# Retention in a three-stage kernel: scores on quarters of TensorE's array, and ahead of the preceding chunk's state part

## The chip, the cores and the metric

The kernel runs on one core of a Trainium2 chip. The metric is the device time of one execution in microseconds (us), as the median of several executions.

## The reference, cut to what matters

Three stages follow one another: a retention layer (2 sequences, 8 heads, 768 steps, head size 64), a mixture of 8 experts with one expert for each token, and a second mixture of 4 experts in which every expert sees every token. The change is in the first.

```python
gamma = 1.0 - 2.0 ** (-5.0 - np.arange(H))
for t in range(S):
    state = gamma[None, :, None, None] * state + np.einsum('bhd,bhe->bhde', k[:, :, t], v[:, :, t])
    y[:, :, t] = scale * np.einsum('bhd,bhde->bhe', q[:, :, t], state)
x = y.transpose(0, 2, 1, 3).reshape(B * S, H * D)
x = moe(x)      # gate: argmax of x @ w_gate; relu(x @ w1[e]) @ w2[e] for the chosen expert
return moe2(x)  # sum over the 4 experts, weighted with the given probabilities
```

All inputs and the output are float32.

## The kernel before, in words

Retention is computed in chunks of 128 steps, 6 of each sequence, 12 in all (NT = 12, NCH = 6). A chunk is numbered i, and c = i % 6 is its place in its sequence. For each chunk there are five pieces of TensorE work, each on all 8 heads:

- S (`st_S`): scores, keys times queries within the chunk. 8 matmuls of 64 x 128 weights against 128 columns: a pair of heads lies on the two halves of the 128 partitions, so the two matmuls of a pair use the two row halves of the array and write two PSUM banks, S_0 and S_1. VectorE multiplies them with the causal mask into `sd` (L251).
- U (`st_U`): keys times values, added up over the chunks of a sequence in one bank that is held (64 columns, 128 x 64 weights, two column halves). ScalarE copies it to `st`, the state (L275). The last chunk of a sequence has no U.
- I (`st_I`): queries times the state of the chunks before, 64 x 64 weights, on quarters of the array, into the banks O_0 and O_1. The first chunk of a sequence has no I.
- O (`st_O`): `sd` times values, 128 x 64 weights (two column halves), added onto I in the same banks. ScalarE copies the two banks to `ot` (L315), GpSimd (POOL) multiplies it with the decay to `xT` (L316); for the last two chunks VectorE does both in one step (L320).
- X (`x_pe`): `xT` times a matrix that transposes it and computes the gate's logits, 128 x 128 weights, into the two held banks x0 and x1. VectorE reduces the logits (L359, L367), ScalarE copies the rest to `xk` (L363) and sends it to memory.

From the logits VectorE finds each token's expert (`x_dve`: `cd` L376, `cm`, `ohs`, `cum`, `ohk`). R (`r_pe`) is two small matmuls that count the tokens ahead of each token; VectorE reads them (`r_dve`: `sel` L403, then `at` L418), and `g_pe` (slot) adds up the table of slots. POOL also makes `vg`, the scaled values (L230).

The loop over `it` issues for each iteration I, U, O and the xT step of chunk it-1, `vg` of chunk it+1, S of chunk it, the loads of chunk it+3, then X of chunk it-2, slot of it-4 and R of it-3 with VectorE's two chains braided: cd, sel, cm, at, ohs, cum, ohk. The engines run in the order in which the program issues (a manual schedule), each at its own pace, and semaphores keep them apart. The loads of q and k (`qk`), k and v (`kv`) go out on SyncE's queue three chunks ahead.

PSUM: O, S and R take their banks from four in turn (`bank`: `banks[nbank[0] % 4]`), so five allocations in an iteration go round four banks; a bank can be written again when its last reader is done. U, slot and X have banks of their own.

A float32 matmul stands in the trace as two weight loads and two matmul records; S of a chunk so has 16 of each. In the order lists below it is one row.

Of the kernel before, what the change touches and what calls it, by code (L numbers as in the profile page):

```python
# [20 lines left out]
P = 128  # L21
# [11 lines left out]
FMAX = 3.4028234663852886e38  # L33
PASS = ((0, 0), (0, 1), (1, 0))
WARM0 = 9
DEPTH = 4
HT = 384
NS = 2 * E2 * 4
# [17 lines left out]
def tile_retention_moe_moe(ctx: ExitStack, tc, qkv, cst, gqt, a1, a2, b1, b2, out, cap):  # L56
# [20 lines left out]
    def bank(name, tag=None):  # L77
        if tag is None:
            tag = banks[nbank[0] % len(banks)]
            nbank[0] += 1  # L80
        return ps[0].tile([P, 512], F32, tag=tag, name=name)

    def warm(n, fill):
        bk = bank("warm")
        for _ in range(n):
            nc.tensor.matmul(out=bk, lhsT=fill[:, 0:P], rhs=fill, start=True, stop=True)
# [20 lines left out]
    def load_w(upto):  # L107
        while nload[0] < min(upto, len(rawof)):
            u = rawof[nload[0]]
            raws[u] = pr.tile([P, 1024], F32, tag="raw", name=f"raw{nload[0]}")  # L110
            nc.sync.dma_start(out=raws[u], in_=wsrc(u))
            nload[0] += 1
# [63 lines left out]
    with ExitStack() as actx:  # L176
# [19 lines left out]
        def load_qk(i):  # L196
            qk_t[i] = pq.tile([P, 2, 512], F32, tag="qk", name=f"qk{i}")
            nc.sync.dma_start(out=qk_t[i], in_=qkv[i, :, 0:1024])

        def load_kv(i):  # L200
            kv_t[i] = pq.tile([P, 2, 512], F32, tag="kv", name=f"kv{i}")
            nc.sync.dma_start(out=kv_t[i], in_=qkv[i, :, 1024:2048])

        def load_gq(c):
            nc.sync.dma_start(out=gqs[:, c], in_=gqt[c])
# [13 lines left out]
        load_kv(2)  # L219
        warm(WARM0, fill)  # L220
        nc.gpsimd.memset(zero, 0.0)
# [5 lines left out]
        def st_v(i):  # L227
            kv = kv_t.pop(i)
            vg = p2.tile([P, 8, HD], F32, tag="vg", name=f"vg{i}", bufs=3)
            nc.gpsimd.tensor_tensor(  # L230
                out=vg, in0=kv[:, 1].rearrange("p (h d) -> p h d", h=8),
                in1=gk[:, i % NCH].rearrange("p (h d) -> p h d", d=1).to_broadcast([P, 8, HD]),
                op=ALU.mult,
            )
            live[i] = {"vg": vg, "k": kv[:, 0]}

        def st_S(i):
            qk = qk_t.pop(i)
            sd = p2.tile([P, 2, 512], F32, tag="sd", name=f"sd{i}")
            live[i].update(sd=sd, q=qk[:, 0])  # L240
            bks = [bank(f"S{i}_{j}") for j in range(2)]
            for hp in range(4):
                cols = slice(hp * P, (hp + 1) * P)
                for j in range(2):
                    r = slice(64 * j, 64 * j + 64)
                    nc.tensor.matmul(  # L246
                        out=bks[j][:, cols], lhsT=qk[r, 1, cols], rhs=qk[r, 0, cols],
                        start=True, stop=True,
                    )
            for j in range(2):  # L250
                nc.vector.tensor_tensor(  # L251
                    out=sd[:, j].rearrange("p (h t) -> p h t", h=4),
                    in0=bks[j].rearrange("p (h t) -> p h t", h=4), in1=causal, op=ALU.mult,
                )
# [3 lines left out]
        def st_U(i):  # L258
            c = i % NCH
            if c == NCH - 1:  # L260
                return
            if c == 0:
                u_ps[0] = bank(f"U{i}", "u")
            u = u_ps[0][:, 0:KD * HD].rearrange("p (a d) -> p a d", a=KD)
            k = live[i].pop("k")
            vg = live[i]["vg"]
            for hp in range(4):
                for j in range(2):
                    h = 2 * hp + j
                    nc.tensor.matmul(  # L270
                        out=u[64 * j:64 * j + 64, hp], lhsT=k[:, h * HD:(h + 1) * HD],
                        rhs=vg[:, h], start=(c == 0 and hp == 0),
                        stop=True, skip_group_check=True,
                    )
            nc.scalar.copy(st[(c + 1) % 2], u)  # L275
# [5 lines left out]
        def st_I(i):  # L281
            c = i % NCH
            live[i]["o"] = [bank(f"O{i}_{j}") for j in range(2)]
            q = live[i].pop("q")
            if c > 0:
                for hp in range(4):
                    for j in range(2):
                        r = slice(64 * j, 64 * j + 64)
                        nc.tensor.matmul(
                            out=o_at(i, hp, j), lhsT=st[c % 2][r, hp],  # L290
                            rhs=q[r, hp * P:(hp + 1) * P], start=(hp < 2), stop=False,
                            skip_group_check=True,
                        )

        def st_O(i):
            d = live[i]
            c = i % NCH
            sd, vg = d.pop("sd"), d.pop("vg")
            for hp in range(4):
                for j in range(2):  # L300
                    nc.tensor.matmul(  # L301
                        out=o_at(i, hp, j), lhsT=vg[:, 2 * hp + j],
                        rhs=sd[:, j, hp * P:(hp + 1) * P], start=(c == 0 and hp < 2), stop=True,
                        skip_group_check=True,
                    )

        def st_x(i):
            d = live[i]
            c = i % NCH
            bks = d.pop("o")  # L310
            xT = p2.tile([P, 512], F32, tag="xT", name=f"xT{i}")
            if i < NT - 2:
                ot = p2.tile([P, 512], F32, tag="ot", name=f"ot{i}")
                for j in range(2):
                    nc.scalar.copy(ot[:, 256 * j:256 * j + 256], bks[j][:, 0:256])  # L315
                nc.gpsimd.tensor_tensor(out=xT, in0=ot, in1=gqs[:, c], op=ALU.mult)  # L316
            else:
                for j in range(2):
                    cols = slice(256 * j, 256 * j + 256)
                    nc.vector.tensor_tensor(  # L320
                        out=xT[:, cols], in0=bks[j][:, 0:256], in1=gqs[:, c, cols], op=ALU.mult
                    )
            d["xT"] = xT
# [98 lines left out]
        def g_pe(i):  # L422
            at = ats.pop(i)
            for b in range(SL // P):
                nc.tensor.matmul(
                    out=slot_ps[:, b], lhsT=at[:, b * P:(b + 1) * P], rhs=ohk[:, i],
                    start=(i == 0 and b == 0), stop=True, skip_group_check=True,
                )
# [6 lines left out]
                        seqs.remove(q)  # L435

        for it in range(NT):
            if it >= 1:
                st_I(it - 1)
                st_U(it - 1)  # L440
                st_O(it - 1)
                st_x(it - 1)
            for i in range(it + 1 if it else 0, min(it + 2, NT)):
                st_v(i)
            st_S(it)
            if it + 3 < NT:
                load_qk(it + 3)
                if it + 2 < NCH:
                    load_gq(it + 2)
                load_kv(it + 3)  # L450
            if it == 5:
                nc.sync.dma_start(out=xd[0:1], in_=zero)
            if it == 2:
                nc.vector.tensor_copy(ub, kc[:, 0:P])
                nc.vector.tensor_copy(ident, iw[:, 0, 0:P])
            if it >= 6:
                load_w(max(nload[0], min(4, it - 5)))
            seqs = []
            if it >= 2:
                x_pe(it - 2)  # L460
                if it >= 4:
                    g_pe(it - 4)
                seqs.append(x_dve(it - 2))
            if it >= 3:
                r_pe(it - 3)
                seqs.append(r_dve(it - 3))
            braid(*seqs)
            if it == 8:
                split_w(0)
# [11 lines left out]
        for b in range(SL // P):  # L481
            nc.gpsimd.indirect_dma_start(
                out=xe0[:, b], out_offset=None, in_=xd[0:1 + NE * P],
# [40 lines left out]
        for ks in (range(2), range(2, KD)):  # L524
# [3 lines left out]
            out=cnt[:, 0], in0=cps, scalar1=float(cap), scalar2=None, op0=ALU.min  # L528
        )
        nc.vector.tensor_tensor(out=cnt[:, 1], in0=cps, in1=cnt[:, 0], op=ALU.subtract)  # L530
        if general:
            nc.vector.tensor_scalar(
                out=nbf, in0=cnt[:, 0], scalar1=float(SM), scalar2=None, op0=ALU.is_gt
            )
            for j in range(1, NB):
                nc.vector.scalar_tensor_tensor(
                    out=nbf, in0=cnt[:, 0], scalar=float(SM + j * P), in1=nbf,
# [200 lines left out]
    def upto(u):  # L738
        ahead = DEPTH + sum(u >= v for v in (5, 7, 29, 31)) - sum(u >= v for v in (W0 - 6, W0 - 5))
        while nsplit[0] <= min(u + ahead, W0 + 3):  # L740
            split_w(nsplit[0])
            nsplit[0] += 1
# [125 lines left out]
    for e in range(E1):  # L868
        x = xet.pop(e)
        hs = []  # L870
        for c in range(4):
# [6 lines left out]
            for ff, k in order:  # L878
# [12 lines left out]
                out=hl, in0=t, scalar=0.0, in1=hh.bitcast(F32), op0=ALU.max, op1=ALU.subtract  # L891
# [413 lines left out]
```

## Time and profile before

| | us |
|---|---|
| median of 3 runs | 744.73 (744.6 to 744.79) |
| the profiled execution | 744.18 |
| its span | 742.4 |
| retention, up to the first expert's product | 68.1 |

The span is what the trace covers. Times in the rows are microseconds from its start. PE stands for TensorE's matmuls and PEld for its weight loads, DVE is VectorE, ACT ScalarE, POOL GpSimd, SP SyncE (SPq its DMA queue). L251 is line 251 of the kernel. A matmul's end is modelled in the trace, so the parts of TensorE's work are told apart here by the start of their first weight load. A row of the timeline merges like instructions that follow one another: start, time that they took together, engine, line, operation, output <- input, array form (weight rows * columns), shapes, count, and in brackets the idle time before it and what ended it.

### The profile page before, as it was taken

The numbers are of one execution on the slowest core, as the hardware profiler recorded it, in microseconds if no ns is written. First come the engines' busy times: TensorE is split into PE (matmuls) and PEld (weight loads), VectorE is DVE, ScalarE is ACT, GpSimd is POOL, SyncE is SP. The second block draws the span as 40 slices with busy tenths as digits, with TensorE's granted clock in tenths as the row PEclk, the third lists the DMA queues.
The fourth block names the chain that finished last, engine by engine and source line by source line (L and its number), as shares of the span: only waits on it lengthen the run. The fifth ranks groups of instructions, "written<-read, shape, count | busy, mean of one in ns | idle before, by whom it ended". The sixth has DMA issues, their size and how long they took to land.

```text
span 742.4 us, 11359 instructions
## 1 busy us (share of the span) xinstructions
PE 727.5 (98%) x4466; PEld 661.8 (89%) x4467; DVE 469.0 (63%) x769; ACT 338.8 (46%) x545; POOL 167.6 (23%) x158
## 2 busy tenths in 40 slices
PE   8998999999999999999999999999999999999996
PEld 5887999999998888899988999889998899988895
DVE  4888889887887935634754645773375454557334
ACT  2334666675665624334443335633445334453341
POOL 3543111222310011222222211213421121111103
PEclk9999999999999999999999999999999999999998
DMA  9985876687561122211113122112221212112002
GB/s 336 409 325 160 298 259 217 214 277 240 201 200 57 40 75 64 103 61 57 57 60 100 41 85 86 58 62 95 100 72 72 86 56 86 58 57 86 29 0 86
DMA packets 27642, 93.22 MB, mean 126 GB/s; under 512 B 3617, under 2 KB 3889, under 8 KB 27586
## 3 DMA queue, kind: packets, MB, share of 16 engines
q1 hardware_dynamic: 23042, 81.79, 31.9%
q0 software_dynamic: 2672, 7.44, 3.2%
q10 hardware_dynamic: 1872, 3.24, 1.1%
q8 instruction: 36, 0.59, 0.3%
q14 instruction: 20, 0.16, 0.1%
HBM read 86.11 MB, written 6.34 MB: 125 GB/s over the span
## 4 chain that ended last, share of the span: by engine, by line
PE 85%; DVE 5%; DMA 5%; ACT 1%; issue 1%; POOL 1%; POOLq 0%; SPq 0%; ACTq 0%; DVEq 0%
PE o L1111 35%; PE a L955 17%; PE m L860 11%; PE b L955 8%; PE m L863 5%; PE bb L955 5%; DMA kv<-qkv 2%; DVE w L125 2%; DMA qk<-qkv 1%; DMA xd<-xk 1%; DVE tsum L889 1%; PE O L301 1%; PE S L246 1%; DMA raw<-a 1%; PE T L701 1%
## 5 line engine op out<-in xcount | busy, mean ns | idle before, releaser
L1111 PE MATMUL o<-w,g_c 128*128 128x512 f32 x1152 | 267.4, 390 | 0.0
L1111 PEld LDWEIGHTS o<-w,g_c 128*128 128x128 f32 x1152 | 215.8, 188 | 43.8
L125 DVE TENSOR_TENSOR w<-raw,w 128x1024 fp32r<-128x1024 f32 x128 | 158.2, 1245 | 16.9 <-ACT w L124 16.7
L955 PE MATMUL a<-X,w 128*128 128x384 f32 x720 | 145.1, 336 | 0.0
L124 ACT CAST w<-raw 128x1024 fp32r<-128x1024 f32 x128 | 132.6, 1048 | 5.9 <-DMA raw<-a 4.2
L990 DVE TENSOR_TENSOR c<-b,c 128x384 f32<-128x384 f32 x30 | 16.7, 558 | 181.2 <-PE b L955 181.2
L955 PEld LDWEIGHTS a<-X,w 128*128 128x128 f32 x720 | 127.3, 188 | 2.6 <-DVE c L990 0.3
L139 POOL TENSOR_TENSOR t<-raw 128x512 f32<-128x512 f32 x28 | 38.8, 1386 | 375.2 <-DMA raw<-b 326.9
L986 ACT COPY c<-a 128x384 f32<-128x384 f32 x60 | 28.7, 479 | 196.4 <-PE a L955 196.4
L860 PE MATMUL m<-h,w 128*128 128x448 f32 x256 | 81.7, 378 | 1.7 <-DVE h L890 1.7
L860 PE MATMUL m<-xet,w 128*128 128x448 f32 x256 | 80.8, 375 | 0.9 <-DVE xet L717 0.9
L971 ACT ACTIVATE g_c<-c 128x384 fp32r<-128x384 f32 x96 | 50.4, 526 | 66.2 <-DVE c L990 64.9
L955 PE MATMUL b<-X,w 128*128 128x384 f32 x360 | 72.0, 334 | 0.0
L863 PE MATMUL m<-h,w 128*128 128x224 f32 x256 | 67.4, 263 | 0.0
L863 PE MATMUL m<-xet,w 128*128 128x224 f32 x256 | 67.4, 263 | 0.0
L955 PEld LDWEIGHTS b<-X,w 128*128 128x128 f32 x360 | 63.5, 188 | 0.0
L975 DVE SCALAR_TENSOR_TENSOR g_c<-c,g_c 128x384 fp32r<-128x384 f32 x96 | 52.9, 552 | 4.0
L860 PEld LDWEIGHTS m<-h,w 128*128 128x128 f32 x256 | 48.0, 187 | 6.1 <-ACT w L124 2.2
L860 PEld LDWEIGHTS m<-xet,w 128*128 128x128 f32 x256 | 48.0, 187 | 4.7 <-PEq L581 1.0
L863 PEld LDWEIGHTS m<-h,w 128*128 128x128 f32 x256 | 48.8, 191 | 0.0
L863 PEld LDWEIGHTS m<-xet,w 128*128 128x128 f32 x256 | 48.8, 190 | 0.0
L955 PE MATMUL bb<-X,w 128*128 128x384 f32 x204 | 41.3, 339 | 0.1
(148 smaller groups left out, 747.1 us busy)
## 6 DMA issues: line engine op xcount, KB each, us to landing
raw<-a SPq DMA_DIRECT2D x64, 512.0 KB, 4.3
raw<-b SPq DMA_DIRECT2D x64, 512.0 KB, 3.5
qk<-qkv SPq DMA_DIRECT2D x12, 512.0 KB, 8.4
kv<-qkv SPq DMA_DIRECT2D x12, 512.0 KB, 8.3
xd<-xk ACTq DMA_DIRECT2D x12, 256.0 KB, 6.6
gqs<-gqt SPq DMA_DIRECT2D x6, 256.0 KB, 7.7
iw<-cst SPq DMA_DIRECT2D x1, 272.0 KB
xe<-xd,gidx POOLq DMA_INDIRECT x16, 4.2
```

The costliest lines, as they stand in the source:

```text
L124: nc.scalar.copy(w[:, 0], r)
L125: nc.vector.tensor_tensor(out=w[:, 1], in0=r, in1=w[:, 0].bitcast(F32), op=ALU.subtract)
L139: eng.tensor_tensor(out=c[:, 0:2], in0=b[:, 2:4], in1=b[:, 1:3], op=sub)
L246: nc.tensor.matmul(out=bks[j][:, cols], lhsT=qk[r, 1, cols], rhs=qk[r, 0, cols], start=True, stop=True,)
L860: nc.tensor.matmul(out=b2, lhsT=w[0], rhs=x, start=first, stop=last, skip_group_check=True)
L863: nc.tensor.matmul(out=b2[:, 0], lhsT=w[1], rhs=x[:, 0], start=False, stop=last, skip_group_check=True)
L955: nc.tensor.matmul(out=bk[:, 0:HT], lhsT=w[:, sw, k], rhs=x[:, sx, k], start=(first and m == 0), stop=(m == len(steps) - 1), skip_group_ch ...
L971: nc.scalar.activation(out=h2[:, 0], in_=src, func=AF.Relu)
L975: nc.vector.scalar_tensor_tensor(out=h2[:, 1], in0=src, scalar=0.0, in1=h2[:, 0].bitcast(F32), op0=ALU.max, op1=ALU.subtract,)
L986: nc.scalar.copy(t, bk[:, 0:HT])
L990: nc.vector.tensor_tensor(out=t, in0=bk[:, 0:HT], in1=t, op=ALU.add)
L1111: nc.tensor.matmul(out=bk, lhsT=h2[:, sh, cols], rhs=w[:, sw, k], start=(q == 0 and m == 0 and (n, t) not in begun), stop=(m == 2), skip_g ...
```

## The change

S is issued as 16 matmuls of 64 x 64 weights instead of 8 of 64 x 128, so that it uses quarters of the array, as I does; each writes half of the partitions of S_0 or S_1. And from it = 4 on S(it) is issued at the head of the iteration, ahead of I, U and O of chunk it-1, instead of behind them. In the first four iterations it stays where it was.

```diff
--- before.py
+++ after.py
@@ -33,6 +33,7 @@
 FMAX = 3.4028234663852886e38
 PASS = ((0, 0), (0, 1), (1, 0))
 WARM0 = 9
+EARLY_S = 4
 DEPTH = 4
 HT = 384
 NS = 2 * E2 * 4
@@ -241,11 +242,13 @@
             bks = [bank(f"S{i}_{j}") for j in range(2)]
             for hp in range(4):
                 cols = slice(hp * P, (hp + 1) * P)
-                for j in range(2):
+                for m in range(4):
+                    o, j = 64 * (m >> 1), m & 1
                     r = slice(64 * j, 64 * j + 64)
                     nc.tensor.matmul(
-                        out=bks[j][:, cols], lhsT=qk[r, 1, cols], rhs=qk[r, 0, cols],
-                        start=True, stop=True,
+                        out=bks[j][o:o + 64, cols],
+                        lhsT=qk[r, 1, hp * P + o:hp * P + o + 64], rhs=qk[r, 0, cols],
+                        start=True, stop=True, skip_group_check=True,
                     )
             for j in range(2):
                 nc.vector.tensor_tensor(
@@ -435,6 +438,8 @@
                         seqs.remove(q)
 
         for it in range(NT):
+            if it >= EARLY_S:
+                st_S(it)
             if it >= 1:
                 st_I(it - 1)
                 st_U(it - 1)
@@ -442,7 +447,8 @@
                 st_x(it - 1)
             for i in range(it + 1 if it else 0, min(it + 2, NT)):
                 st_v(i)
-            st_S(it)
+            if it < EARLY_S:
+                st_S(it)
             if it + 3 < NT:
                 load_qk(it + 3)
                 if it + 2 < NCH:
```

In the order lists the number behind a name is the chunk (S10_0 is the first score bank of chunk 10), the number behind _ a buffer's. TensorE around iteration 10 before: the end of R, then I of chunk 9 (O9 written from qk9 and st).

```order
323 L329 LDWEIGHTS onesb_74
324 L329 MATMUL R6_836<-cum_79,onesb_74 128x8 [waits Activation_49]
325 L330 LDWEIGHTS ub_73
326 L330 MATMUL R6_836<-ohs_80,ub_73 128x8 [waits DVE_49]
327 L289 MATMUL O9_0_850<-qk9_571,st1_114 64x128 [waits Activation_49]
328 L289 MATMUL O9_1_851<-qk9_571,st1_114 64x128 [waits DVE_49]
```

Further on in the same iteration, before: the end of O of chunk 9 and the start of S of chunk 10.

```order
341 L301 MATMUL O9_0_850<-sd9_807,vg9_715 64x128
342 L301 MATMUL O9_1_851<-sd9_807,vg9_715 64x128
343 L301 MATMUL O9_0_850<-sd9_807,vg9_715 64x128
344 L301 MATMUL O9_1_851<-sd9_807,vg9_715 64x128
345 L246 MATMUL S10_0_885<-qk10_647 128x128 [waits DMAHW3_49,PE_49]
346 L246 MATMUL S10_1_886<-qk10_647 128x128 [waits DVE_49]
```

The same two places of iteration 10 after the change. TensorE behind R:

```order
403 L332 LDWEIGHTS onesb_74
404 L332 MATMUL R6_916<-cum_79,onesb_74 128x8 [waits DVE_49]
405 L333 LDWEIGHTS ub_73
406 L333 MATMUL R6_916<-ohs_80,ub_73 128x8
407 L248 MATMUL S10_0_931<-qk10_711 64x128 [waits DMAHW3_49,DVE_49]
408 L248 MATMUL S10_1_932<-qk10_711 64x128 [waits Activation_49]
```

and at the end of S of chunk 10:

```order
420 L248 MATMUL S10_1_932<-qk10_711 64x128
421 L248 MATMUL S10_0_931<-qk10_711 64x128
422 L248 MATMUL S10_1_932<-qk10_711 64x128
423 L292 MATMUL O9_0_951<-qk9_627,st1_114 64x128 [waits Activation_49]
424 L292 MATMUL O9_1_952<-qk9_627,st1_114 64x128 [waits DVE_49]
425 L292 MATMUL O9_0_951<-qk9_627,st1_114 64x128
```

S has moved from behind O to behind R, with twice the instructions, and I follows it. The semaphores that the first matmuls wait for have moved too: the second matmul of S waited for VectorE and now waits for ScalarE; the second of I waits for VectorE, as before.

VectorE in iteration 11, before: the end of iteration 10's chain, then xT of chunk 10 out of the O banks, sd of chunk 11 and the reduction of X.

```order
134 L391 TENSOR_SCALAR ohk_81<-ohs_80,kc_75 128x8
135 L320 TENSOR_TENSOR xT10_954<-O10_0_927,gqs_110 128x256 [waits DMAHW3_49,PE_49,Pool_49]
136 L320 TENSOR_TENSOR xT10_954<-O10_1_928,gqs_110 128x256 [waits PE_49]
137 L251 TENSOR_TENSOR sd11_957<-S11_0_958,cdec_109 128x512 [waits PE_49]
138 L251 TENSOR_TENSOR sd11_957<-S11_1_959,cdec_109 128x512 [waits PE_49]
139 L359 TENSOR_REDUCE lgs_82<-X9_0_972 128x8 [waits PE_49]
```

and after:

```order
134 L394 TENSOR_SCALAR ohk_81<-ohs_80,kc_75 128x8
135 L254 TENSOR_TENSOR sd11_1015<-S11_0_1016,cdec_109 128x512 [waits PE_49]
136 L254 TENSOR_TENSOR sd11_1015<-S11_1_1017,cdec_109 128x512 [waits PE_49]
137 L323 TENSOR_TENSOR xT10_1063<-O10_0_1036,gqs_110 128x256 [waits PE_49,Pool_49]
138 L323 TENSOR_TENSOR xT10_1063<-O10_1_1037,gqs_110 128x256 [waits PE_49]
139 L362 TENSOR_REDUCE lgs_82<-X9_0_1068 128x8 [waits PE_49]
```

The sd products of chunk 11 now stand ahead of xT of chunk 10. In the other iterations the order on VectorE, ScalarE, POOL and SyncE is unchanged.

## Rows read from the trace of the kernel before

**Rows 1.** First part of the page: busy time of each engine, share, instructions.

```profile
PE 727.5 (98%) x4466; PEld 661.8 (89%) x4467; DVE 469.0 (63%) x769; ACT 338.8 (46%) x545; POOL 167.6 (23%) x158
```

**Rows 2.** By stage: stretch, length, PE, PEld, DVE, ACT, POOL busy, clock, DMA share.

```profile
19.72:22.95 3.23, 3.23 (x67) 2.77 (x65) 3.13 (x13) 1.66 (x5) 2.29 (x3) 1.00 1.03 400
27.39:31.36 3.97, 3.97 (x63) 3.46 (x61) 3.72 (x14) 1.12 (x4) 2.53 (x3) 1.00 1.03 402
31.36:36.09 4.73, 4.32 (x63) 3.79 (x61) 4.36 (x15) 1.29 (x4) 2.28 (x2) 1.00 1.03 414
40.77:45.21 4.44, 4.44 (x77) 3.93 (x76) 3.15 (x15) 1.87 (x5) 1.87 (x2) 1.00 1.03 415
45.21:50.17 4.96, 4.86 (x78) 4.11 (x76) 4.36 (x15) 2.31 (x8) 2.61 (x3) 1.00 1.02 409
50.17:54.61 4.44, 4.44 (x79) 3.93 (x77) 3.88 (x16) 1.02 (x3) 2.09 (x2) 1.00 0.38 148
```

**Rows 3.** Timeline of one iteration, TensorE's weight loads.

```profile
51.38 0.42 PEld L289 LDWEIGHTS O<-qk,st 64*64 64x64 f32 x16
...
51.97 0.55 PEld L270 LDWEIGHTS U<-vg,kv 128*64 128x64 f32 x16 [0.17 <-issue]
...
52.44 0.91 PEld L301 LDWEIGHTS O<-sd,vg 128*64 128x64 f32 x16
...
53.52 0.97 PEld L246 LDWEIGHTS S<-qk 64*128 64x128 f32 x16 [0.17 <-issue]
...
54.61 0.99 PEld L344 LDWEIGHTS X<-iw,xT 128*128 128x128 f32 x8
...
55.52 0.21 PEld L425 LDWEIGHTS <-at 128*128 128x128 f16 x2
...
55.81 0.42 PEld L289 LDWEIGHTS O<-qk,st 64*64 64x64 f32 x16
```

**Rows 4.** Timeline behind O of chunk 9: S, ScalarE and POOL.

```profile
49.08 0.97 PEld L246 LDWEIGHTS S<-qk 64*128 64x128 f32 x16 [0.17 <-issue]
...
49.20 0.65 ACT L315 COPY ot<-O 128x256 f32<-128x256 f32 x2 [0.18 <-PE O L301]
...
49.99 1.27 POOL L316 TENSOR_TENSOR xT<-ot,gqs 128x512 f32<-128x512 f32 x1 [1.57 <-ACT ot L315]
...
51.22 1.04 POOL L230 TENSOR_TENSOR vg<-kv,cdec 128x512 f32<-128x512 f32 x1
```

**Rows 5.** Timeline from 32.5 to 35 us, then two VectorE rows at 56 us.

```profile
32.56 1.28 POOL L316 TENSOR_TENSOR xT<-ot,gqs 128x512 f32<-128x512 f32 x1 [1.61 <-issue]
...
32.94 0.92 DVE L367 CUSTOM_DVE_ANT_0 lgs<-lgs,part 128x8 f32<-128x8 f32 x1
...
33.80 1.04 POOL L230 TENSOR_TENSOR vg<-kv,cdec 128x512 f32<-128x512 f32 x1
...
33.91 0.96 DVE L376 SCALAR_TENSOR_TENSOR cd<-lgs,mxs,kc 128x8 f32<-128x8 f32 x1
...
34.78 0.15 DVE L403 CUSTOM_DVE_ANT_0 sel<-R,ohs 128x8 f32<-128x8 f32 x1
...
35.00 0.96 PEld L246 LDWEIGHTS S<-qk 64*128 64x128 f32 x14 [0.60 <-DVE ranks L403]
...
56.20 0.17 DVE L367 CUSTOM_DVE_ANT_0 lgs<-lgs,part 128x8 f32<-128x8 f32 x1
...
56.41 0.23 DVE L376 SCALAR_TENSOR_TENSOR cd<-lgs,mxs,kc 128x8 f32<-128x8 f32 x1
```

**Rows 6.** Timeline rows of a load and of vg; last, a wait of SyncE's queue.

```profile
20.22 0.33 SPq L205 DMA_DIRECT2D gqs<-gqt  x1
...
26.56 1.04 POOL L230 TENSOR_TENSOR vg<-kv,cdec 128x512 f32<-128x512 f32 x1 [1.95 <-DMA kv<-qkv]
...
29.91 1.04 POOL L230 TENSOR_TENSOR vg<-kv,cdec 128x512 f32<-128x512 f32 x1 [0.64 <-DMA kv<-qkv]
...
SPq L111 <- DVEq L581: 15.4, 1, 15.4
```

## The prediction

> **What bounds the kernel now.** I read the first part of the page first: TensorE is busy 98% of the span [rows 1], so time is won or lost where TensorE waits or does work that can go. The change touches only the retention loop, so next I cut that loop into its iterations, from the start of one X product to the next [rows 2]: the eight iterations in which the scores will move (it = 4 to 11) last 3.97 to 4.96 us (of the first only 3.23, from the start of I, are shown); in the worst of them TensorE is busy 4.32 of 4.73 us, and the granted clock is 1.00 (2.4 GHz) in all. The DMA share is full (1.02 to 1.03) until 50.17 us. Then I took one undisturbed iteration apart by TensorE's weight loads, whose first start is the start of a part [rows 3]: I 51.38, U 51.97, O 52.44, S 53.52, X 54.61, slot and R 55.52, the next I 55.81. So TensorE bounds this stage, except where something that it waits for comes later; those places I looked for last.
>
> **What the change removes.** In X eight records of 136 columns take 0.91 us [rows 3], 114 ns each with no gap, so a record of 128 columns streams in 107 ns and one of 64 in 54 ns. S before is 16 records in two row halves: 8 x 107 = 0.86 us of stream, and it takes 1.09. O: 16 records in two column halves, 0.86 of 1.08. I: 16 records on quarters, 0.43 of 0.59. U: 16 records of 64 columns in two halves, 0.43 of 0.47, and O after it has the same form. So a change of form costs 0.16 to 0.23 us and the same form costs 0.04. Afterwards S is 32 records on quarters, 32 / 4 x 107 = 0.86 us, the same stream, and I follows it in the same form: S 0.86, I 0.59, U 0.47, O 1.08, X 0.91, slot and R 0.29 make 4.20 us against 4.44 [rows 2, 3]. If nothing waited, each of eight iterations would gain about 0.23 us. S on quarters in it = 0 to 3 changes neither the number of forms nor the stream; I cost it at nothing, with bounds of -0.1 and +0.2 us in each for a form that the trace shows only in I.
>
> The smaller instructions have a rule against them. In I eight matmul instructions had their weights loaded within 0.42 us [rows 3], 53 ns each, which is what S on quarters needs. The Trainium skill, TensorE: Matmul & The Clock Gate (section Wait — 56ns, not 53.3ns?) says that with hardware decode off the sequencer spends about 62 ns on each matmul; by that figure, an estimate, sixteen would take 0.99 us instead of 0.86. The row speaks against it, and below that time lies under a wait anyway.
>
> **What the change adds: an earlier meeting with a bank.** S, O and R draw from four banks in turn, five in an iteration, and each reuses the bank of four allocations ago. Before, the order O0 O1 S0 S1 R makes S1 reuse R's bank of the iteration before; that bank is free when VectorE has read it (sel, L403). After, the order S0 S1 O0 O1 R makes O1 reuse it, and the first to write O1 is the second matmul of I. Before, U, O and (mostly) I lay between R and the wait, 0.59 + 0.47 + 1.08 = 2.14 us; now only S does, 0.86. Behind the waiting matmul stand the rest of I, U, O and X, in order on TensorE. The other new waits are met early: S0 on sd of the chunk before, S1 on the first copy of O to ot (both copies are over 0.77 us after the end of O [rows 4], and S comes 1.20 after it).
>
> When does sel run? Take t0 as the start of X, which now is also the end of O. Copies of O to ot start 0.12 us after it (49.08 to 49.20), POOL's xT product 0.91 after it, and vg 1.23 later, 1.04 long [rows 4]: POOL works from t0 + 0.91 to t0 + 3.18 without a gap. VectorE's chain to sel begins when X ends at about t0 + 1.0 to 1.2: two reductions out of PSUM, the sum L367 (two SBUF inputs), cd L376, sel. What POOL does to these is shown at 32.56 to 35.00 [rows 5]: the sum L367, 0.17 us where POOL rests, took 0.92 and ended at 33.86, as POOL's xT did (33.84); cd, 0.23 otherwise, took 0.96 and ended at 34.87, as vg did (34.84); sel followed, and S, the present user of the bank, went on at 35.00, 0.16 after vg. Before the change this is the exception, since VectorE's chain is mostly run behind POOL's pair; after it, O ends just as X starts, so the pair covers the chain in every iteration. TensorE then goes on at t0 + 3.18 + 0.16 = t0 + 3.34, where I was ready at t0 + 0.91 + 0.29 + 0.86 = t0 + 2.06: a wait of 1.28 us. I (0.59), U and O behind it give a next X at t0 + 5.48, **1.04 us later than now**, wait and gain taken together.
>
> That VectorE and POOL lock each other out is also a rule of the Trainium skill, SBUF — State Buffer (section Who interferes with whom): a VectorE instruction with two SBUF inputs against a GpSimd one that reads SBUF, and whoever issues first has the ports for its whole instruction. The trace agrees on L367 and L376; by the second half of the rule a VectorE chain that starts ahead of xT would not wait at all, and that is the second rival below.
>
> **The sum, iteration by iteration** (starts of X before are the bounds of [rows 2]).
> it = 4: S(4) could start at 19.72 [rows 2] but its qk lands at 20.22, since the DMA issued then waits for the same semaphore as S(4) [rows 6]. 20.25 + 0.86 + 0.59 + 0.47 + 1.08 = X at 23.25, 0.3 late.
> it = 5: kv of chunk 5 lands at 26.56 [rows 6], so POOL has only xT in VectorE's way; sel ends near 25.9, I goes on at 25.95, X at 28.1, 0.7 late.
> it = 6: kv of chunk 6 is there at 29.91 [rows 6], xT runs 29.0 to 30.3 and vg right behind it to 31.3; I goes on at 31.5. Chunk 5 has no U: X at 33.2, 1.8 late.
> it = 7: chunk 6 has no I, so U runs ahead of the wait and O meets it at 33.2 + 3.34 = 36.55: X at 37.6, 1.5 late (before lost 0.9 us in this place itself [rows 5]).
> it = 8 to 11: 5.48 each, X at 43.1, 48.6, 54.0 and 59.5, against 40.77, 45.21, 50.17 and 54.61. The iteration from 45.21 lost 0.5 us before, which now lies under the wait.
> Past the loop the same instructions follow; VectorE has chunk 11's sd behind it by then, which I count as -0.1 us. 59.5 - 54.61 - 0.1 = **+4.7 us**. Nothing later takes it up: SP's weight loads wait for the branch after retention (15.4 us [rows 6]), so they and the experts move along. The profiled execution took 744.18 us (span 742.4), the median is 744.73: 744.73 + 4.7 = 749.4.
>
> **Rivals.**
> *No wait, faster.* sel is done when I gets there, say because POOL's pair falls elsewhere. Then the iterations take 4.20 us (3.7 and 3.6 for the chunks without U and I), X(9) starts at 51.8, also because the losses of before in the iterations from 31.36 and 45.21 [rows 2] go: -2.8, 741.9 us. For it: VectorE no longer has sd between X and its chain. Against it: xT starts at t0 + 0.91 and the sum L367 can't before t0 + 1.0. Decides: whether L367 starts before xT. Chance 0.12.
> *Only one POOL instruction in the way.* cd slips in between xT and vg, or vg waits for its kv: cd ends at t0 + 2.18 + 0.03 + 0.05 + 0.23, TensorE goes on at t0 + 2.62, iterations take 4.76. Stepping as above, X(9) starts at 55.2: +0.6, 745.3 us. Against it: at 33.80 vg began before xT's row had ended. Chance 0.18.
> *The wait, and a slower clock.* TensorE would idle 1.28 of 5.48 us. The most idle iteration of before, 0.41 of 4.73, kept 1.00 [rows 2]. At 1.2 GHz, half the rate, I, U, O and X (3.05 us) would take twice their time, 3 us more in each of five iterations: 764 us. Chance 0.04.
> *The bank is not the one I say,* or S on quarters runs its four parts one after another (32 x 107 = 3.4 us instead of 0.86): the latter adds up to 2.6 us in each of twelve chunks, partly under the wait, 760 to 770 us; the former gives the times of the first rival or of none. I's rows [rows 3] and the wait put down to L403 in S before [rows 5] speak against both. Chance 0.04.
>
> **How the numbers follow.** My forecast, the wait in nearly every iteration, has 0.62: 749.4 us, between 747 (POOL's pair escapes twice) and 752 (S on quarters and a DMA lane cost 2 us more). The range goes down to 744.8 to take in the second rival: 744.8 to 752.0, with 0.12 below and 0.08 above. About 0.2%, 1.5 us, is what a measurement of this kernel can tell from no change: faster below 743.2, slower above 746.2. Faster 0.12, same 0.17 (the second rival), slower 0.71.
>
> **What would show it.** In the profile after, the weight loads of I should pause behind its first rows, put down to L403's counterpart, by about 1.3 us in it = 6 and 8 to 10; iterations of 5.4 to 5.5 us from 43 us on; L367's and L376's counterparts near 1 us each; S with 32 records in 0.86 us and no pause between S and I's first record; the first expert's product near 72.8 instead of 68.1 us. The forecast is wrong if L367 stays at 0.17 us there, or if TensorE has no idle time ahead of I.

## The result, and the profile after

The change makes the kernel slower. The median went from 744.76 us (6 runs, 744.6 to 745.31) to 750.35 us (6 runs, 748.52 to 752.36): a ratio of 1.0076, 95% interval 1.0059 to 1.0092. The profiled execution of the changed kernel took 748.52 us with a span of 746.8 us, 4.4 us more than the span of before.

In the code of after all line numbers of the retention are three higher: S is L248, I L292, the first sum L370, cd L379, sel L406. The rows of the changed kernel that answer to [rows 2] are the iterations from one start of X to the next (columns as there):

```profile
19.02:23.55 4.53, 4.53 (x94) 3.99 (x90) 4.15 (x16) 1.02 (x3) 2.84 (x3) 1.00 1.04 408
23.55:28.29 4.74, 4.64 (x94) 4.01 (x92) 3.57 (x14) 1.76 (x5) 2.58 (x3) 1.00 1.04 408
28.29:33.29 5.00, 4.41 (x78) 3.54 (x77) 4.49 (x16) 1.39 (x4) 2.27 (x2) 1.00 1.02 407
33.29:37.65 4.36, 4.16 (x78) 3.54 (x76) 3.53 (x14) 1.80 (x6) 2.28 (x2) 1.00 1.03 410
37.65:42.96 5.31, 4.64 (x93) 4.02 (x92) 4.90 (x16) 1.70 (x5) 2.27 (x2) 1.00 1.03 413
42.96:48.44 5.48, 4.64 (x95) 4.02 (x93) 4.31 (x14) 2.81 (x6) 2.27 (x2) 1.00 1.03 411
48.44:53.92 5.48, 4.64 (x94) 4.01 (x92) 5.10 (x16) 1.71 (x5) 2.28 (x2) 1.00 0.60 215
53.92:59.41 5.49, 4.64 (x95) 4.02 (x93) 4.19 (x14) 1.76 (x5) 2.28 (x2) 1.00 0.12 48
```

The reader is to see two things: the last three iterations have one length, whether the DMA share is 1.03 or 0.12, and TensorE is idle for some 0.84 us in each of them, at a granted clock of 1.00. Where TensorE is idle stands in the timeline of its weight loads, one iteration of it (answering to [rows 3]):

```profile
42.96 0.99 PEld L347 LDWEIGHTS X<-iw,xT 128*128 128x128 f32 x8 [0.17 <-issue]
...
44.17 0.86 PEld L248 LDWEIGHTS S<-qk 64*64 64x64 f32 x32
44.99 0.24 PEld L292 LDWEIGHTS O<-qk,st 64*64 64x64 f32 x2
46.30 0.42 PEld L292 LDWEIGHTS O<-qk,st 64*64 64x64 f32 x14 [1.07 <-DVE ranks L406]
46.89 0.55 PEld L273 LDWEIGHTS U<-vg,kv 128*64 128x64 f32 x16 [0.17 <-issue]
...
48.44 0.99 PEld L347 LDWEIGHTS X<-iw,xT 128*128 128x128 f32 x8 [0.17 <-issue]
```

S takes 0.86 us for 32 records, and I starts behind it with no gap. Its first matmul (two records) goes through, since it writes O0; the second, the first that writes O1, waits for sel. That is the bank of R. Why sel is late stands on VectorE and POOL, an iteration earlier, where the rows answer to those of 32.56 to 35.00 in [rows 5]:

```profile
38.40 1.27 POOL L319 TENSOR_TENSOR xT<-ot,gqs 128x512 f32<-128x512 f32 x1 [1.93 <-ACT ot L318]
...
39.09 0.60 DVE L370 CUSTOM_DVE_ANT_0 lgs<-lgs,part 128x8 f32<-128x8 f32 x1
...
39.63 1.04 POOL L231 TENSOR_TENSOR vg<-kv,cdec 128x512 f32<-128x512 f32 x1
...
39.74 0.96 DVE L379 SCALAR_TENSOR_TENSOR cd<-lgs,mxs,kc 128x8 f32<-128x8 f32 x1
...
40.62 0.15 DVE L406 CUSTOM_DVE_ANT_0 sel<-R,ohs 128x8 f32<-128x8 f32 x1
...
40.83 0.42 PEld L292 LDWEIGHTS O<-qk,st 64*64 64x64 f32 x14 [0.91 <-DVE ranks L406]
```

The sum L370 ends with xT and cd ends with vg; sel and I follow within 0.2 us.

### The profile page after: what moved, and what is told of

It is laid out like the page before. It is cut to its first block, busy times and chain, and to the rows that moved or that the text cites. A ratio compares the mean times of both kernels' runs of the same rounds, so it can differ in the third digit from the quotient of the medians.

```text
span 746.8 us, 11743 instructions
## 1 busy us (share of the span) xinstructions
PE 728.0 (97%) x4658; PEld 661.3 (89%) x4659; DVE 471.4 (63%) x769; ACT 340.5 (46%) x545; POOL 164.6 (22%) x158
## 4 chain that ended last, share of the span: by engine, by line
PE 84%; DVE 7%; issue 2%; DMA 2%; ACT 2%; POOL 1%; POOLq 0%; DVEq 0%; SPq 0%; ACTq 0%
PE o L1117 34%; PE a L961 17%; PE m L866 10%; PE b L961 8%; PE m L869 5%; PE bb L961 5%; DVE w L126 2%; PE X L347 2%; PE O L304 1%; DMA raw<-a 1%; DVE tsum L895 1%; DVE cd L379 1%; PE O L292 1%; DVE lgs L370 1%; DMA kv<-qkv 1%
```

## The experiments

Each kernel was timed beside the kernel before on the same chip (744.99, 745.07 and 745.16 us in three groups), so ratios are to that. Where no interval is given, there is one time and a trace. The theory is that of the prediction: I waits for the bank that R and O1 share, and VectorE frees it late because POOL's xT and vg hold up two of its reductions.

**Quarters at the old place of S.**

```diff
-EARLY_S = 4
+EARLY_S = 12
```

> S on quarters of the array in all chunks, but S stays behind O in every iteration, as before. Theory (the loss is the wait for R's bank behind sel, which comes from the new place of S): the banks are drawn in the old order and the number of array forms is the old one, so 744.7 us within 0.5, S 0.86 to 1.1 us a chunk. Rival 1 (S in twice as many, half as large instructions is what costs): near 750 us with the place of S unchanged.

744.92 us, ratio 0.9999 (0.999 to 1.0008). One iteration of its weight loads:

```profile
40.98 0.99 PEld L347 LDWEIGHTS X<-iw,xT 128*128 128x128 f32 x8 [0.17 <-issue]
...
44.33 0.86 PEld L248 LDWEIGHTS S<-qk 64*64 64x64 f32 x32 [0.17 <-issue]
45.36 0.99 PEld L347 LDWEIGHTS X<-iw,xT 128*128 128x128 f32 x8 [0.17 <-issue]
```

Quarters by themselves cost nothing that the time shows. The loss lies in the place of S.

**S early, on halves.**

```diff
-                for m in range(4):
-                    o, j = 64 * (m >> 1), m & 1
+                for j in range(2):
...
-                        out=bks[j][o:o + 64, cols],
-                        lhsT=qk[r, 1, hp * P + o:hp * P + o + 64], rhs=qk[r, 0, cols],
-                        start=True, stop=True, skip_group_check=True,
+                        out=bks[j][:, cols], lhsT=qk[r, 1, cols], rhs=qk[r, 0, cols],
+                        start=True, stop=True,
```

> S moved ahead from chunk 4 on, but on halves of the array as before. Theory: the same wait in I, which also covers the extra change of form between S and I, so X of chunk 9 starts near 59.4 us and the time is that of the changed kernel, 750.4 us within 1.5; the idle time of I put down to sel shrinks from 1.3 to about 1.1 us an iteration. Rival 1 (quarters cost): 744.7 us or less.

752.04 us, ratio 1.0102 (1.0086 to 1.0118). From X to X:

```profile
44.61 0.99 PEld L345 LDWEIGHTS X<-iw,xT 128*128 128x128 f32 x8 [0.17 <-issue]
...
45.81 0.97 PEld L247 LDWEIGHTS S<-qk 64*128 64x128 f32 x16
46.91 0.19 PEld L290 LDWEIGHTS O<-qk,st 64*64 64x64 f32 x2
47.96 0.42 PEld L290 LDWEIGHTS O<-qk,st 64*64 64x64 f32 x14 [0.86 <-DVE ranks L404]
...
50.09 0.99 PEld L345 LDWEIGHTS X<-iw,xT 128*128 128x128 f32 x8 [0.17 <-issue]
```

The iteration is 5.48 us again. The change of form is there (S starts at 45.81, I 1.10 later instead of 0.82), and the wait is shorter by 0.21 us, 0.86 for 1.07: what the form costs or saves vanishes under the wait. The time itself missed what I had expected by little: it is 1.7 us above the changed kernel's, and I had allowed 1.5. In the traces X starts 1.65 us later than in the changed kernel (50.09 against 48.44), and that has grown ahead of this iteration. The first X of the early kind starts 1.07 us later (20.09 against 19.02), since U of chunk 2 waits 1.86 us for vg and vg for its load, against 1.20 in the changed kernel, and the step before was late by the rest. The iteration from 24.48 us lasts 5.46 instead of 4.74 us, since here vg follows xT at once and the full wait for ranks is there (0.85 against 0.34 us). That these two come from the halves is not shown; both hang on when a load lands.

**sel ahead of the reductions.** VectorE reads R's bank before it starts the chain that POOL holds up.

```diff
-                x_pe(it - 2)
+                x_pe(it - 2, False)
...
                 seqs.append(r_dve(it - 3))
+                next(seqs[-1])
+            if it >= 2:
+                x_reduce(it - 2)
             braid(*seqs)
```

> The changed kernel, with VectorE's sel moved ahead of the reductions of X and of L370 and cd in each iteration; banks, POOL and TensorE's order untouched. Theory: sel has one input in PSUM and runs about 0.15 us behind R, so I no longer waits, iterations take 4.2 to 4.3 us from 43 us on, X of chunk 9 starts at 52 to 53 us and the time is 741.5 to 743 us, less than before. Rival 1 (quarters) and rival 2 (the early S costs for another reason, its loads or its other banks): 749 to 751 us, iterations still 5.4 us.

747.27 us, ratio 1.0031 (1.0019 to 1.0044): better than the changed kernel, but not what I expected. No matmul of I waits for ranks any more, and the undisturbed iterations are 4.21 to 4.22 us. What eats the gain are pauses of TensorE that the trace puts down to nothing ("issue"), in the midst of a row of like matmuls: 3.6 us in four pauses, and X of chunk 9 starts at 56.40 us where I had expected 52 to 53. A second execution of this kernel was to show whether they are tied to places in the program:

> The changed kernel with sel ahead of the reductions, a second execution of it with its own trace. If the three pauses of 0.9 to 1.4 us on TensorE are tied to places in the instruction stream, they stand at the same matmuls again (U of iteration 4 behind 15 records, S of iteration 8 behind 13, I of iteration 9 behind 15). If they are chance, they stand elsewhere or are fewer; the span is then 743 to 746. No wait on ranks in either case.

747.22 us. They stand at the same matmuls again: S of iteration 8 pauses behind 13 records and I of iteration 9 behind 15 in both executions. The second has one pause more, at 30.13 us, and that of U in iteration 4 is shorter (0.44 for 1.44 us). Two of the pauses in the weight loads of that second execution:

```profile
42.40 0.41 PEld L248 LDWEIGHTS S<-qk 64*64 64x64 f32 x13
43.80 0.52 PEld L248 LDWEIGHTS S<-qk 64*64 64x64 f32 x17 [0.98 <-issue]
...
48.60 0.47 PEld L292 LDWEIGHTS O<-qk,st 64*64 64x64 f32 x15
50.28 0.13 PEld L292 LDWEIGHTS O<-qk,st 64*64 64x64 f32 x1 [1.21 <-issue]
```

The pauses come every 6 to 7.5 us, and so do, until 48 us, the packets of one of the two DMA queues that carry instructions. A stretch of 0.25 us of the DMA view shows one (queue: packets, MB, share of 16 engines in the stretch; here 47.75 to 48.00 us):

```profile
q8 instruction: 1, 0.02, 25.9%
```

The table sets the start of each packet's stretch of 0.25 us beside the pauses of 0.3 us or more in S, I, U and O that are put down to issue. The packet itself starts up to 0.25 us later than its stretch:

| kernel | stretch with a packet of q8 starts at | pause ends at |
|---|---|---|
| sel first | 21.0, 41.5, 48.0 | 23.80, 44.09, 50.39 |
| sel first, second execution | 20.25, 27.5, 33.75, 41.0, 47.75 | 22.84, 30.13, 36.29, 43.80, 50.28 |
| changed kernel | 27.75 | 30.26 |
| changed kernel, second execution | 27.75 | 30.30 |
| quarters, old place | 20.5 | 23.15 |

Each pause ends 2.4 to 2.8 us behind the start of a packet's stretch, in these kernels and in three of the four with quarters that follow. The fourth, vg ahead of xT, has one pause of 0.33 us that doesn't. In the kernels with S on halves (before, and the three on halves among the experiments) no pause ends so. The pauses also stand at fixed counts of TensorE's records. The trace counts the matmuls and weight loads up to the end of a pause (columns as in [rows 2]; second execution, first two pauses):

```profile
0.00:22.84 22.84, 18.17 (x346) 13.65 (x348) 10.63 (x36) 5.83 (x16) 8.96 (x14) 1.00 0.93 349
0.00:30.13 30.13, 25.11 (x471) 19.75 (x473) 15.88 (x56) 8.86 (x26) 13.05 (x17) 1.00 0.96 363
```

That is 694 and 944 records. The next three pauses end at 1197, 1451 and 1701, so the five are 250 to 254 records apart, and every other pause of the table ends within three records of one of these counts. Over the whole span the changed kernel has 9317 such records and 37 packets of q8, which makes 252 records for a packet. My reading is that TensorE has run out of instructions and goes on when the next block is there: S on quarters takes 16 matmul instructions where halves take 8, and without a wait TensorE gets to a block's end sooner. In the changed kernel its wait for sel leaves the block time to land, so of these pauses only one shows there.

**vg ahead of xT on POOL.**

```diff
-                st_x(it - 1)
             for i in range(it + 1 if it else 0, min(it + 2, NT)):
                 st_v(i)
+            if it >= 1:
+                st_x(it - 1)
```

> The changed kernel, with POOL's vg of the next chunk issued ahead of xT, so that only xT stands behind the end of O. Theory (POOL holds up L370 and then cd): only L370 is held up, cd runs at once, TensorE goes on at about 2.6 us after the start of X instead of 3.34, iterations of 4.7 to 4.8 us from 43 us on; 745 to 747.5 us, since vg waits for its load in the first of these iterations and xT behind it. Rival 3 (sel is late by its place on VectorE behind X, not by POOL): iterations of 5.4 to 5.5 us, 750 us or more.

754.37 us, ratio 1.0136 (1.012 to 1.0151). The iterations stay at 5.48 us:

```profile
48.82 1.28 POOL L319 TENSOR_TENSOR xT<-ot,gqs 128x512 f32<-128x512 f32 x1 [3.20 <-ACT ot L318]
...
49.35 0.77 DVE L370 CUSTOM_DVE_ANT_0 lgs<-lgs,part 128x8 f32<-128x8 f32 x1
...
50.06 1.04 POOL L231 TENSOR_TENSOR vg<-kv,cdec 128x512 f32<-128x512 f32 x1
...
50.16 0.96 DVE L379 SCALAR_TENSOR_TENSOR cd<-lgs,mxs,kc 128x8 f32<-128x8 f32 x1
51.05 0.15 DVE L406 CUSTOM_DVE_ANT_0 sel<-R,ohs 128x8 f32<-128x8 f32 x1
...
51.26 0.42 PEld L292 LDWEIGHTS O<-qk,st 64*64 64x64 f32 x14 [1.08 <-DVE ranks L406]
```

The edit doesn't do what I wanted. Ahead of xT in POOL's queue, the vg of one iteration waits for nothing and starts as soon as the xT of the iteration before ends, so the two still run as a pair. It tells the theories apart in nothing, though the time is what the rival expected; that POOL's two instructions are to blame needed the next but two. The 4 us above the changed kernel have another cause, early in the loop, where vg waits for its load and now holds up xT and so X:

```profile
17.61 1.33 PEld L347 LDWEIGHTS X<-iw,xT 128*128 128x128 f32 x8 [4.09 <-POOL xT L319]
```

In the changed kernel this X starts at 13.70 us.

**The kernel before, with sel ahead of the reductions.** The edit is the same, on the kernel before.

> The kernel before with one edit: VectorE makes sel (the step that frees the bank of R) ahead of the two reductions, which POOL's xT and vg hold up, instead of behind cd. Theory (the bank wait is what POOL's pair makes, and the kernel before has only little of it, in the scores S of iterations 7 and 8, 0.60 us in the row at 35.00 of [rows 5], and otherwise stands at 4.2 to 4.44 us an iteration): the waits of S on ranks are gone, the time goes down by 0.6 to 1.2 us, to 743.5 to 744.4. Rival (the earlier sel costs as much behind it, since xk and the reductions come 0.2 us later): no change, 745. Rival (making sel early brings the same pauses on TensorE, put down to nothing, as in the early-quarters kernel with sel first, since they come with TensorE running without waits): 745.5 to 747, with pauses of 0.8 us or more in the rows of U, S or I.

744.82 us, ratio 0.9994 (0.9986 to 1.0003): no change. S no longer waits for ranks, and the X that began at 36.09 us [rows 2] begins at 35.35. Then R waits 0.5 us for ot and I 0.37 us for sd, and the gain is gone; two later waits, 0.34 us for sd and 0.45 of X for xk, stand in the kernel before too, as 0.34 and 0.30. The first expert's product starts at 68.59 us (68.10 before). Taking the bank wait of before away was worth nothing to the total, as the rival said, but by other waits than the rival named.

**Halves, early, with sel ahead of the reductions.** The edit of the second kernel and that of the third together. (The 16 that halves have fewer are records; that is 8 matmuls.)

> The changed kernel with S early, but on halves (16 matmuls fewer an iteration than on quarters), and sel ahead of the reductions. No matmul should wait for ranks. Theory (the three pauses of 0.9 to 1.4 us in the kernel with early quarters and sel first come with the longer row of TensorE instructions that the quarters bring, 8 more matmuls in each chunk): no such pauses, iterations of 4.4 us (one change of form more than with quarters), 743.5 to 744.5. Rival (the pauses come with TensorE running without waits, whatever the form): two or three pauses of about 1 us and 746.5 to 748. Rival (the place of S ahead of I costs by itself, through its bank or through sd): iterations of 4.8 us and 747 or more, with a wait named in the rows.

746.54 us, ratio 1.0026 (1.0015 to 1.0037). Iterations without a pause, of 4.43 us (40.83 to 45.26) and 4.44 (50.86 to 55.30), came as expected, but not the total. One iteration loses 1.1 us in another place:

```profile
47.03 0.17 PE L330 MATMUL R<-cum,onesb 128*128 128x8 f16 x1 [0.54 <-DVE sd L252]
47.03 0.10 PEld L331 LDWEIGHTS <-ub 128*128 128x128 f16 x1 [0.61 <-issue]
...
47.63 0.97 PEld L247 LDWEIGHTS S<-qk 64*128 64x128 f32 x16 [0.50 <-DVE sd L252]
```

R, the fifth allocation, takes the bank of S0 of its own iteration, as in every kernel with S ahead, and waits until VectorE has made sd of it. So with the bank's other owner served, this owner is the next to be late, in the iteration in which VectorE also makes the first split of the weights (1.23 us, just ahead of sd). Only the absence of the pauses speaks for the reading of the instruction blocks here, not the time.

**vg on VectorE from chunk 7 on.**

```diff
             for i in range(it + 1 if it else 0, min(it + 2, NT)):
-                st_v(i)
+                if i < 7:
+                    st_v(i)
...
             braid(*seqs)
+            if 7 <= it + 1 < NT:
+                st_v(it + 1, nc.vector)
```

> The changed kernel, but from chunk 7 on vg is made on VectorE, behind the last step of the iteration's routing, instead of on POOL. POOL then has only xT in the way of the reductions. Theory (each of POOL's two instructions holds up one reduction of VectorE): the first reduction still ends with xT, cd takes its bare time of some 0.2 us instead of 0.96, sel is done 0.7 us earlier, I's wait goes down from 1.09 to 0.3 to 0.4 us and the iterations from 5.48 to 4.7 to 4.8 from iteration 8 on: 747 to 748. Rival (sel is late by its place behind the reductions and VectorE's own queue, not by POOL): iterations stay at 5.48 or grow by VectorE's vg, 750 to 753. Rival (VectorE's vg makes sd late and S's banks with it): a wait of S on sd of 0.5 us or more.

747.17 us, ratio 1.0033 (1.0022 to 1.0045).

```profile
48.12 1.27 POOL L319 TENSOR_TENSOR xT<-ot,gqs 128x512 f32<-128x512 f32 x1 [3.68 <-ACT ot L318]
...
48.82 0.60 DVE L370 CUSTOM_DVE_ANT_0 lgs<-lgs,part 128x8 f32<-128x8 f32 x1
...
49.46 0.23 DVE L379 SCALAR_TENSOR_TENSOR cd<-lgs,mxs,kc 128x8 f32<-128x8 f32 x1
49.49 0.75 PEld L292 LDWEIGHTS O<-qk,st 64*64 64x64 f32 x16
...
49.61 0.16 DVE L406 CUSTOM_DVE_ANT_0 sel<-R,ohs 128x8 f32<-128x8 f32 x1
```

With xT alone in the way L370 still takes 0.60 us, but cd takes its bare 0.23, and the iterations from 37.52 to 56.89 us last 4.75, 4.94, 4.94 and 4.74: the 4.76 that the prediction's second rival was worked out with. In the last of them I waits 0.35 us for ranks and goes on at 54.76, t0 + 2.61; the rival had t0 + 2.62. In the first, S has waited 0.31 us for sd, which covers most of it; in the two in between pauses of 0.55 and 0.36 us, ending 2.4 and 2.6 us behind the start of a packet's stretch, come on top. This shows what the second of POOL's two instructions costs: some 0.7 us an iteration.

**R in a bank of X.** All of the changed kernel, sel as late as there, but R writes into free columns of X's second bank.

```diff
-                x_pe(it - 2)
+                xb = x_pe(it - 2, False)
...
-                r_pe(it - 3)
+                r_pe(it - 3, xb)
                 seqs.append(r_dve(it - 3))
+            if it >= 2:
+                x_reduce(it - 2)
...
-            bk = bank(f"R{i}")
+            r = bank(f"R{i}")[:, 0:8] if bk is None else bk[:, 272:280]
```

> The changed kernel, all of it, with one thing else: in the loop R is written into eight free columns (272 to 280) of the second bank of X instead of a bank of the round of four, so that S0, S1, O0 and O1 keep the round to themselves and O1 follows O1 of the iteration before. sel stays behind cd, as late as in the changed kernel. Theory (I waits for sel only because R and O1 share a bank): no wait on ranks in I, iterations of 4.2 us where TensorE does not pause, and, with the pauses that the kernel with sel first has (each ending some 2.5 us behind the start of a transfer of TensorE's instructions), 745.5 to 747.5; were there no such pauses, 741.5 to 743. Rival (sel's lateness reaches TensorE by another way than the bank, through at, the slots or the ohs of the next routing): iterations of about 5.4 us with another wait in the rows of X, R or the slots, 749 to 751. Rival (X's bank now comes free late): a wait of X on ranks, 0.3 us or more in each iteration, 747 to 749.

745.79 us, ratio 1.0013 (1.0003 to 1.0023).

```profile
37.20 0.99 PEld L351 LDWEIGHTS X<-iw,xT 128*128 128x128 f32 x8 [0.17 <-issue]
...
39.22 0.48 PEld L292 LDWEIGHTS O<-qk,st 64*64 64x64 f32 x16
...
39.40 0.96 DVE L384 SCALAR_TENSOR_TENSOR cd<-lgs,mxs,kc 128x8 f32<-128x8 f32 x1
...
40.28 0.15 DVE L411 CUSTOM_DVE_ANT_0 sel<-X,ohs 128x8 f32<-128x8 f32 x1
...
41.41 0.99 PEld L351 LDWEIGHTS X<-iw,xT 128*128 128x128 f32 x8 [0.17 <-issue]
```

This is the plainest of the experiments. cd is held up for 0.96 us as before and sel is as late as before, and I runs its 16 records at once, a microsecond ahead of sel. The iteration is 4.21 us, the sum of the prediction without a wait (4.20). So sel reaches TensorE through the bank and no other way. What is left of the loss: pauses that end 2.6 to 2.8 us behind the start of a packet's stretch (at 22.56, 30.34 and 36.51 us: 0.41, 1.03 and 0.53 us), and S waiting for sd (0.53 and 0.41 us at 47.45 and 48.04).

**The weights' loads behind the retention.** The kernel with sel first; the loads of the first weights and their first split move behind the loop.

```diff
-            if it >= 6:
-                load_w(max(nload[0], min(4, it - 5)))
...
-            if it == 8:
-                split_w(0)
+        load_w(5)
+        split_w(0)
         st_I(NT - 1)
```

> The changed kernel with sel ahead of the reductions, and the loads of the first weights and their first split taken out of the retention's loop and put behind it (their order stays). The DMA engines then have only q, k, v and xd to move from iteration 6 on. The total is longer, since the first expert's weights come late; only the rows up to 55 us count. Theory (TensorE's pauses are waits for its next block of instructions, and the block comes late because the DMA engines are full): the pauses near 44 and 50 us are below 0.3 us or gone, those near 23 and 30 us stay. Rival (the block is asked for too late, whatever the traffic): the pauses near 44 and 50 us stay at 0.9 to 1.2 us, some 2.5 us behind the start of the transfer.

748.69 us, of which the end is not comparable. The pauses near 44 and 50 us stay, at 0.80 and 1.08 us (0.89 and 1.00, 0.98 and 1.21 in the two executions of sel first). But the experiment didn't bring the condition about that it was for (length, busy times of PE, PEld, DVE, ACT and POOL, clock, DMA share, GB/s):

```profile
46.00:48.00 2.00, 2.00 (x32) 1.79 (x31) 0.82 (x5) 0.75 (x3) 0.55 (x1) 1.00 1.05 420
48.00:50.00 2.00, 1.28 (x47) 1.04 (x39) 1.93 (x9) 0.65 (x2) 1.73 (x2) 1.00 0.76 297
```

q, k, v and xd alone fill the DMA engines until 48 us, and the packet of the second pause starts ahead of that, in the stretch from 47.5 us. Only the rest of the 2.6 us from there to the pause's end saw some room, and the pause was no shorter. Whether the block is late because of the traffic or because it is asked for late stays open.

**The changed kernel again.**

> The changed kernel once more, for a second trace of it: its times lie between 748.5 and 752.4, and the trace on record is of the fastest. If the wait of I on ranks is what the change costs in each execution, iterations from 8 to 11 are again 5.4 to 5.5 us with waits of 1.0 to 1.1 us. What the longer executions have on top should stand as pauses on TensorE put down to nothing, outside those iterations or in the first ones.

750.0 us, span 748.2. The waits of I and the iterations are those of the first trace, 5.47 to 5.49 us from 43.23 to 59.67 us, and the first expert's product starts at 73.02 instead of 72.72 us. The other 1.1 us lie behind it, not where I had expected them; of that, 0.7 us are TensorE's waits for the experts' h (line waited for: us in total, times, longest; the second trace, then the first):

```profile
PE m L866 <- DVE h L896: 2.5, 3, 1.5
```

```profile
PE m L866 <- DVE h L896: 1.8, 3, 1.1
```

None of the kernels that I ran is measurably faster than the kernel before.

## Why the prediction was right

The forecast was 749.4 us, the range 744.8 to 752.0; measured 750.35. Of the rivals none came true in the changed kernel; the iteration of the second came true in the kernel with vg on VectorE, though not its total (747.17 us, where it had 745.3).

**The bank and the wait: right.** TensorE was to go on at t0 + 3.34; in the iteration from 42.96 us it does at 46.30, which is t0 + 3.34. I was ready at 44.99, t0 + 2.03 (predicted 2.06), and its first matmul used 0.24 of what had been put down as wait, so the idle time reads 1.07 to 1.09 us. The kernel with R in X's bank shows that the bank carries it, the ones with sel first that sel's place sets it.

**The iterations: right.** The starts of X for it = 4 to 11 were given as 23.25, 28.1, 33.2, 37.6, 43.1, 48.6, 54.0 and 59.5; they are 23.55, 28.29, 33.29, 37.65, 42.96, 48.44, 53.92 and 59.41. The largest miss is it = 4: there a wait of 0.16 us for ranks already stands at 21.39 us, where I had only counted the late qk. The first expert's product was put at 72.8 and starts at 72.72.

**What the change removes: right.** S on quarters takes 0.86 us and meets I without a change of form. Sixteen matmul instructions in 0.86 us are 54 ns each. The 62 ns that the Trainium skill (TensorE: Matmul & The Clock Gate, section Wait — 56ns, not 53.3ns?) gives for hardware decode off don't show here; whether it was off, no run shows. Nor did quarters in it = 0 to 3 cost anything that the total shows (744.92 with all twelve on quarters).

**POOL's hold on VectorE: right in its end, wrong in one duration.** I expected about 1 us for both the sum and cd. cd takes 0.96, the sum only 0.60 to 0.76, because it starts later in xT's run; it ends when xT ends all the same, and that is what sets sel. With vg taken off POOL cd falls from 0.96 to 0.23 us. The Trainium skill, SBUF — State Buffer (section Who interferes with whom), says that of such a pair whichever issues first keeps the other blocked for its whole instruction; the trace agrees. (The case that VectorE's chain starts ahead of xT is the prediction's first rival, not the second, as is said there.)

**The sum: right for the profiled execution.** The terms of the sum add up to 4.79 us, which the prediction wrote as 4.7; the trace has 4.80 at X of chunk 9 and 4.62 at the first expert's product. Put on the profiled execution, 744.18 + 4.7 = 748.9, and 748.52 was measured; the span grew by 4.4. The median is 0.95 us above the forecast. The second trace shows where such an execution is longer: 0.3 us ahead of the experts and 1.1 us in them. From the first expert's product to the end I read 674.3 us before, 674.1 and 675.2 in the two traces of the changed kernel, 675.2 in the first of sel first and 673.7 in the kernel before with sel first, though these instructions are the same in all. Whether the change moves that stage or the executions merely differ there isn't settled.

**What the rival "no wait" missed.** I had put 741.9 us on it, from iterations of 4.20 us (its steps bring X of chunk 9 to 51.6, not 51.8 us, which changes little). Three kernels took the wait away, and they gave 745.79, 746.54 and 747.27. The iteration of 4.21 us is real, but the term lacked two things that only show once the wait is gone: TensorE's pauses with quarters, and S and R waiting for sd. Had the rival decided the outcome, the time would have been 4 to 5 us off and "faster" the wrong sign.

## What to carry to other kernels

Where tiles draw from a small round of banks, moving one step changes which earlier owner each later step must wait for: write out the owner of each bank four (or however many) allocations back before and after, and ask when that owner's last reader runs, on whichever engine it is. The cheap cure was not to speed the reader up but to take the small, late-read tile out of the round (5.48 to 4.21 us an iteration here, though the total, 745.79 us, was still no better than before). And when a wait is removed, don't price the gain by the sum of the rest: look at what the wait covered, the readers of the other banks and the supply of instructions among them.

## What the runs showed of the hardware

TensorE's pauses weren't in my picture. With S on quarters and no wait, it stops for up to 1.4 us in the midst of like matmuls, at places that repeat between executions of one kernel (43.80 and 44.09, 50.28 and 50.39 us), each time until 2.4 to 2.8 us after the start of the stretch in which a packet of the instruction queue starts; until 48 us these packets are 6 to 7.5 us apart. The pauses stand some 250 records apart, and there is one packet for 252 records. That the one causes the other is inferred from these times and counts and from the halves, where the pauses are missing; it wasn't shown by moving a packet.

The waits of 1.07 to 1.09 us in each iteration left the granted clock at 1.00, its 2.4 GHz. In the kernel with vg ahead of xT, behind the idle stretch of 4.09 us that ended at 17.61 us, it stood at 0.50, which is 1.2 GHz, from 18.60 to 21.60 us, and TensorE worked in that stretch without a break. So what the rival "the wait, and a slower clock" names does happen here, but the wait that came with the change did not bring it about.
